# Copying the keys and summaries of every query tile on ScalarE instead of VectorE

## The chip, the cores and the metric

The kernel runs on one core of a Trainium2 chip. The metric is the device time of one execution in microseconds (us), taken as a median over runs. Differences are judged against that median. Engines are named as the profile names them: PE is TensorE's matmuls and PEld its weight loads, DVE is VectorE, ACT is ScalarE, POOL is GpSimd, SP is SyncE, whose queue issues most DMAs.

## The reference

Three layers run one after the other: an attention over a local window plus block summaries, a gated feed-forward layer, and a mixture of eight experts with a fixed capacity.

```
k_sum = k.reshape(B, H, nb, block, D).max(axis=3)          # block = 32
v_sum = v.reshape(B, H, nb, block, D).mean(axis=3)
scores_l = scale * q @ k^T, kept where |pos_q - pos_k| < 16, else -1e9
scores_s = scale * q @ k_sum^T + log(block)
a = softmax(concat[scores_l, scores_s])                    # over both kinds of keys
x = a @ concat[v, v_sum]

h = x @ w_in                                               # 512 -> 2048
x = (h * clip(h + 3, 0, 6) / 6) @ w_out                    # 2048 -> 512

logits = x @ w_gate                                        # 8 experts, 192 tokens each
assigned by falling logit, each expert up to its capacity
out[tokens of e] = relu(x @ w1[e]) @ w2[e]
```

B = 2, H = 8, 768 positions, head size 64, all in float32. The change touches the attention only.

## The kernel before, in words

**Query tiles.** The 1536 tokens are cut into twelve tiles of 128 queries, n = 0 to 11; tiles 0 to 5 are batch 0. For each batch the keys are transposed once into `kT` (two heads on 128 partitions, four such pairs, 768 positions), and `ks` holds the 24 block maxima. A tile is worked in two groups of 64 queries. Each group sees a window of 96 keys (its own 64 and 16 on each side) and all 24 summaries, 120 keys together. `window(n)` puts these 120 columns side by side into `kw` for each pair of heads and each group: two copies of keys of 4 x 96 columns a partition, and two of summaries of 4 x 24. At the ends of a batch (tiles 0, 5, 6 and 11) one window is cut short, its copy is smaller, and a memset fills the rest. Tile 0 is prepared in two halves of two pairs each. `qT` and `kw` have one buffer each.

**One step of the attention** handles half the heads of a tile (h = 0 or 1). `front` multiplies `qT` by `kw` on PE (line 372), then DVE adds the mask and takes the maximum, four times (line 380), and scales it (line 382). `soften` takes four exponentials on ACT (line 392, each with the sum of its row), DVE adds a small number to the sums and inverts them (lines 394 and 395), and POOL scales the weights `A` (line 396). Two steps later `turn` transposes `A` on PE (line 404) and ACT takes the result out of PSUM (line 406); `values` multiplies by the values on PE (line 419), and ACT and DVE split the result into an upper and a lower part of `x` (lines 437 and 77). In the second step of a tile the next one is prepared: `q_prep` transposes its queries on PE (line 338) and ACT copies `qT` (line 340), and then `window` fills `kw`.

**The first feed-forward product** (`gemm1`) runs for units of three tiles. Per block of 128 hidden columns twelve matmuls (lines 587 to 589) fill one of two PSUM banks; ACT takes the relu (line 590), DVE the gate (line 601), and that frees the bank. The weights come as 8-byte floats; DVE makes 4-byte floats of them in three instructions per block (line 268), ACT copies the upper part (line 285) and POOL subtracts (line 286). These conversions run during the first unit.

**What sets the order.** Instructions are issued to each engine in the order of the program and executed in that order. `drive` merges several generators: it always lets the one go on that is least far by planned costs (the numbers after `yield`), between a start and an end given as shares. First the preparation of batch 0 with tiles 0 to 2 beside the first conversions; then `gemm1` of unit u beside the attention of unit u + 1; after that the second product, the routing and the experts, in which no query tile is prepared.

Of the kernel before, what the change touches and what calls it, by code (L numbers as in the profile page):

```python
# [11 lines left out]
AF = mybir.ActivationFunctionType  # L12
# [7 lines left out]
WIN = QG + 2 * W  # L20
# [67 lines left out]
def build(ctx, tc, q, k, v, w_in, w_out, w_gate, w1, w2, out):  # L88
    nc = tc.nc
    PE, ACT, DVE, POOL, SP = nc.tensor, nc.scalar, nc.vector, nc.gpsimd, nc.sync  # L90
# [46 lines left out]
    kT = att.tile([128, HP, S], FT)  # L137
    ks = att.tile([128, HP, NB], FT)
# [205 lines left out]
    def window(n, hps=slice(0, HP)):  # L344

        i = n % 6
        kw = fr[n][1][:, hps]
        if i in (0, 5):
            for g in range(2):
                lo = i * 128 + g * QG - W  # L350
                a, z = max(lo, 0), min(lo + WIN, S)
                if z - a < WIN:
                    DVE.memset(kw[:, :, g, :W] if a > lo else kw[:, :, g, WIN - W:WIN], 0.0)
                DVE.tensor_copy(kw[:, :, g, a - lo:z - lo], kT[:, hps, a:z])
        else:
            for g in range(2):
                lo = i * 128 + g * QG - W
                DVE.tensor_copy(kw[:, :, g, :WIN], kT[:, hps, lo:lo + WIN])
        for g in range(2):
            DVE.tensor_copy(kw[:, :, g, WIN:], ks[:, hps])  # L360

    def front(n, h, after):
        b, i = divmod(n, 6)
        qT, kw = fr[n]
        A = Abuf[(2 * n + h) % (LAG + 1)]
        sp = [bank(0), bank(1)]
        for pr in range(2):
            hp = 2 * h + pr
            for g in range(2):
                for s in range(2):  # L370
                    r, c = slice(64 * s, 64 * s + 64), slice(QG * g, QG * g + QG)
                    PE.matmul(sp[s][c, pr * KEYS:(pr + 1) * KEYS], qT[r, hp, c], kw[r, hp, g], start=True, stop=True)
        if after:
            q_prep(n + 1)
        mk = mask[:, 0 if i == 0 else 2 if i == 5 else 1]
        sm = att.tile([128, 4, 4], FT, name="sm", bufs=2)
        for pr in range(2):
            for s in range(2):
                c = 2 * pr + s
                DVE.tensor_tensor_reduce(out=A[:, c], in0=sp[s][:, pr * KEYS:(pr + 1) * KEYS], in1=mk, scale=1.0,  # L380
                                         scalar=-3e38, op0=OP.add, op1=OP.max, accum_out=sm[:, 0, c:c + 1])
        DVE.tensor_scalar(sm[:, 1], sm[:, 0], -SCALE, None, op0=OP.mult)
        if after:
            window(n + 1)
        later.append((A, sm))
# [57 lines left out]
    def halves():  # L443
        for n in range(NT):
            b, i = divmod(n, 6)
            if b and i == 0:
                for g in range(2):
                    vsum(b, g)
                yield from kprep(b)
                zone()  # L450
                q_prep(n)
                window(n)
                yield 2400
# [286 lines left out]
    def prologue():  # L740
        for g in range(2):
            for i, c in enumerate(kprep_first(g)):
                yield c
                if g == 1 and i == 1:
                    yield next(attention)
                warm(1)
            warm((2, 8)[g])
            q_prep(0, range(2 * g, 2 * g + 2))
            window(0, slice(2 * g, 2 * g + 2))
            yield 450  # L750
            if g == 0:
                yield next(attention)
        yield from attend_unit(0)
# [71 lines left out]
    g = [0.0] + [RATIO ** i for i in range(J - 1)]  # L825
# [396 lines left out]
```

## Time and profile before

| what | value |
|---|---|
| median of 3 runs | 602.12 us (601.99 to 603.04) |
| profiled execution | 600.1 us, its span 598.2 us |
| busy, PE | 551.2 us, 92% of the span |
| busy, DVE | 400.6 us, 67% |
| busy, ACT | 288.8 us, 48% |
| busy, POOL | 178.2 us, 30% |
| mean granted TensorE clock | 0.981 of full |

The shares are averages over stages with different limits, so they don't tell which engine a stage waits for. The span runs from the first instruction to the last; the 1.9 us beside it lie around them. The query tiles are prepared between 8.9 us and 176 us of the span, twelve times. In a timeline a row is one instruction, or several of a kind merged, with its start, its duration, its engine and its line; in brackets stands how long the engine had been idle before and what it waited for. Neighbours on an engine overlap a little, so the distance between two starts is shorter than the first one's duration.

### The profile page before, as it was taken

What the parts mean: (1) busy time and instruction counts of PE and PEld (TensorE: products, weight loads), DVE (VectorE), ACT (ScalarE), POOL (GpSimd) and SP (SyncE); (2) the same over time, 40 slices, a digit from 0 to 9 for tenths busy, and PEclk for the clock granted to TensorE, in tenths of its full rate; (3) what the DMA queues carried; (4) which work ended last, traced back from release to release, by engine and by line L of the source; (5) the groups of instructions that cost most, each with busy time, mean ns of one, the idle gap of its engine ahead of it and who ended that gap; (6) DMA issues with size and microseconds to landing.
All of it is one profiled execution on the core that took longest, in us unless ns stands there. A gap on an engine that the chain in (4) does not pass through costs nothing.

```text
span 598.2 us, 10910 instructions
## 1 busy us (share of the span) xinstructions
PE 551.2 (92%) x3811; PEld 466.8 (78%) x3811; DVE 400.6 (67%) x1215; ACT 288.8 (48%) x694; POOL 178.2 (30%) x204
## 2 busy tenths in 40 slices
PE   7679778989999999899999898899999999999994
PEld 6558667878899999776687676678789889988883
DVE  6898994555534399961037787762588888888880
ACT  4376453435645455641131131133577677776760
POOL 1444648111111034662243434545101101110111
PEclk9879998989999999999999999999999999999998
DMA  9985981202210245330060000003579879887811
GB/s 204 253 194 147 257 200 33 49 18 64 58 39 1 72 142 175 112 93 1 1 201 11 0 2 2 0 19 142 168 219 283 231 241 283 265 253 240 253 61 32
DMA packets 102400, 75.06 MB, mean 125 GB/s; under 512 B 47488, under 2 KB 88448, under 8 KB 101952
## 3 DMA queue, kind: packets, MB, share of 16 engines
q1 hardware_dynamic: 100352, 67.96, 41.8%
q0 software_dynamic: 1984, 6.32, 2.9%
q8 instruction: 32, 0.52, 0.4%
q14 instruction: 32, 0.26, 0.1%
HBM read 67.55 MB, written 6.71 MB: 124 GB/s over the span
## 4 chain that ended last, share of the span: by engine, by line
PE 39%; issue 27%; DVE 23%; DMA 4%; POOL 3%; ACT 2%; SPq 1%; POOLq 0%; ACTq 0%; DVEq 0%
PE bank L587 7%; PE bank L588 6%; PE bank L589 6%; DVE t L268 5%; PE bank L704 3%; PE bank L705 3%; PE bank L706 3%; DVE big L889 3%; POOL out_dram L1025 2%; PE bank L894 2%; DVE x L529 2%; PE bank L613 2%; DMA t<-in_q_dram 2%; PE bank L419 1%; DVE A L380 1%
## 5 line engine op out<-in xcount | busy, mean ns | idle before, releaser
L587 PE MATMUL bank<-x,wh 128*128 128x384 f32 x256 | 92.4, 361 | 9.5 <-DVE t L601 9.3
L295 DVE TENSOR_TENSOR wl<-t,wh 128x1024 fp32r<-128x1024 f32 x64 | 77.0, 1221 | 20.5 <-ACT wh L294 18.1
L681 ACT ACTIVATE work<-t 128x384 fp32r<-128x384 f32 (+2 forms) x80 | 36.4, 459 | 107.5 <-PE bank L705 101.2
L589 PE MATMUL bank<-x,wl 128*128 128x384 f32 x256 | 87.4, 341 | 0.8 <-POOL wl L286 0.8
L588 PE MATMUL bank<-x,wh 128*128 128x384 f32 x256 | 87.1, 340 | 0.8 <-DVE x L77 0.8
L590 ACT ACTIVATE t<-bank,three 128x384 f32<-128x384 f32 x64 | 37.2, 581 | 94.1 <-PE bank L589 94.0
L682 POOL TENSOR_TENSOR tlx<-t,work 128x384 fp32r<-128x384 f32 (+1 forms) x52 | 56.8, 1094 | 84.2 <-ACT work L681 84.2
L704 PE MATMUL bank<-wh,work 128*128 128x512 f32 x192 | 78.0, 406 | 2.0 <-DVE t L601 2.0
L706 PE MATMUL bank<-wh,tlx 128*128 128x512 f32 x192 | 75.3, 392 | 0.1
L705 PE MATMUL bank<-wl,work 128*128 128x512 f32 x192 | 74.8, 390 | 0.0
L1050 PE MATMUL bank<-x,wh 128*128 128x384 f32 x256 | 73.7, 360 | 0.5 <-DVE x L976 0.5
L294 ACT ACTIVATE wh<-t 128x1024 fp32r<-128x1024 f32 x64 | 65.6, 1047 | 0.0
L1052 PE MATMUL bank<-x,wl 128*128 128x192 f32 x256 | 64.2, 251 | 0.0
L601 DVE SCALAR_TENSOR_TENSOR t<-t,bank 128x384 f32<-128x384 f32 x64 | 34.7, 548 | 40.0 <-ACT t L590 40.0
L396 POOL TENSOR_TENSOR A<-A,sm 128x480 f32<-128x480 f32 x24 | 24.2, 1010 | 119.0 <-ACT at L406 74.9
L587 PEld LDWEIGHTS bank<-x,wh 128*128 128x128 f32 x256 | 48.9, 191 | 13.4 <-DVE t L601 5.9
L1025 POOL DMA_INDIRECT out_dram<-t,idx x16 | 14.9, 930 | 141.6 <-DVE t L1074 136.1
L588 PEld LDWEIGHTS bank<-x,wh 128*128 128x128 f32 x256 | 49.1, 192 | 1.4 <-DVE x L77 1.4
L589 PEld LDWEIGHTS bank<-x,wl 128*128 128x128 f32 x256 | 48.9, 191 | 1.2 <-POOL wl L286 1.2
L1052 PEld LDWEIGHTS bank<-x,wl 128*128 128x128 f32 x256 | 48.9, 191 | 0.3
L1066 PE MATMUL bank<-wh,t 128*128 128x512 f32 x128 | 49.0, 392 | 0.0
L1050 PEld LDWEIGHTS bank<-x,wh 128*128 128x128 f32 x256 | 48.1, 188 | 1.2 <-DVE x L976 0.8
(182 smaller groups left out, 1088.9 us busy)
## 6 DMA issues: line engine op xcount, KB each, us to landing
t<-in_moe_w_dram SPq DMA_DIRECT2D x128, 256.0 KB
t<-in_moe_w_in_dram SPq DMA_DIRECT2D x16, 512.0 KB
big<-in_moe_w_out_dram SPq DMA_DIRECT2D x16, 512.0 KB
VW<-in_v_dram SPq DMA_DIRECT2D x20, 192.0 KB
t<-in_v_dram SPq DMA_DIRECT2D x4, 768.0 KB
t<-xs SPq DMA_DIRECT2D x8, 258.0 KB
raw<-in_q_dram SPq DMA_DIRECT2D x8, 256.0 KB
t<-in_k_dram SPq DMA_DIRECT2D x12, 128.0 KB
```

The source lines that it names most:

```text
L294: ACT.activation(hi, x, AF.Copy)
L295: DVE.tensor_tensor(lo, x, hi.bitcast(FT), op=OP.subtract)
L587: PE.matmul(p, wh[:, kk, :], xh[:, kk, :], start=kk == 0, stop=False)
L588: PE.matmul(p, wh[:, kk, :], xl[:, kk, :], start=False, stop=False)
L589: PE.matmul(p, wl[:, kk, :], xh[:, kk, :], start=False, stop=kk == KD - 1)
L682: (DVE if placed[0] else POOL).tensor_tensor(ths[i][1], t, ths[i][0].bitcast(FT), op=OP.subtract)
L704: PE.matmul(acc[j], th[:, c], WH[s], start=f == 0, stop=False)
L705: PE.matmul(acc[j], th[:, c], WL[s], start=False, stop=False)
L706: PE.matmul(acc[j], tl[:, c], WH[s], start=False, stop=f == NF - 1)
L1050: PE.matmul(p, a[:, kk, :], xt[:, kk].rearrange("p c s -> p (c s)"), start=kk == 0, stop=False, skip_group_check=True)
L1052: PE.matmul(p[:, :CAP], b[:, kk, :], xt[:, kk, 0, :], start=False, stop=kk == KD - 1, skip_group_check=True)
L1066: PE.matmul(p, x, w, start=m == 0 and i == 0, stop=m == NM - 1 and i == 2)
```

## The change

The copies that fill `kw` move from DVE to ACT, with the same sources, targets and sizes. The memset of a window that is cut short stays on DVE. Nothing else is edited.

```
                 if z - a < WIN:
                     DVE.memset(kw[:, :, g, :W] if a > lo else kw[:, :, g, WIN - W:WIN], 0.0)
-                DVE.tensor_copy(kw[:, :, g, a - lo:z - lo], kT[:, hps, a:z])
+                ACT.activation(kw[:, :, g, a - lo:z - lo], kT[:, hps, a:z], AF.Copy)
         else:
             for g in range(2):
                 lo = i * 128 + g * QG - W
-                DVE.tensor_copy(kw[:, :, g, :WIN], kT[:, hps, lo:lo + WIN])
+                ACT.activation(kw[:, :, g, :WIN], kT[:, hps, lo:lo + WIN], AF.Copy)
         for g in range(2):
-            DVE.tensor_copy(kw[:, :, g, WIN:], ks[:, hps])
+            ACT.activation(kw[:, :, g, WIN:], ks[:, hps], AF.Copy)
```

The order of PE's instructions is the same as before, and DVE's and ACT's differ in these copies alone. ACT's queue at the start, from the second half of tile 0 to the exponentials that follow the preparation of tile 1 (`kT` are the transposed keys, `bank_...` PSUM tiles, `A` the weights):

```order
 L308 ACTIVATE kT<-bank_223 128x2x2x128
 L340 ACTIVATE qT<-bank_241 128x256
+L354 ACTIVATE kw<-kT 128x2x80
+L354 ACTIVATE kw<-kT 128x2x96
+L360 ACTIVATE kw<-ks 128x2x24 x2
 L340 ACTIVATE qT<-bank_263 128x512
+L358 ACTIVATE kw<-kT 128x4x96 x2
+L360 ACTIVATE kw<-ks 128x4x24 x2
 L392 ACTIVATE A_90,sm<-A_90,sm 128x120 x4
```

Tile 1's copies now stand behind its `qT` and ahead of the exponentials of the step before it.

ACT's queue at the preparation of tile 3, where line 285 is the upper part of a converted weight block:

```order
 L406 ACTIVATE at<-bank_459 120x512
 L340 ACTIVATE qT<-bank_477 128x512
+L358 ACTIVATE kw<-kT 128x4x96 x2
+L360 ACTIVATE kw<-ks 128x4x24 x2
 L285 ACTIVATE wh<-t 128x512
 L392 ACTIVATE A_91,sm<-A_91,sm 128x120 x4
```

The four copies come ahead of the weight copy and the exponentials.

DVE's queue at the preparation of tile 5, the last one of batch 0, with the end of a step's maxima ahead and a conversion behind:

```order
 L380 ISA sm 128x1
 L382 TENSOR_SCALAR sm<-sm 128x4
-L354 COPY kw<-kT 128x4x96
 L353 MEMSET kw 128x4x16
-L354 COPY kw<-kT 128x4x80
-L360 COPY kw<-ks 128x4x24 x2
 L268 TENSOR_SCALAR t<-t 128x512
 L268 SCALAR_TENSOR_TENSOR t<-t 128x512 x2
```

After the scaled maxima only the memset is left ahead of the conversion.

## Rows read from the trace of the kernel before

**Rows 1.** Busy time by stretch: us, PE, PEld, DVE, ACT, POOL, PEclk, DMA share, GB/s.

```profile
48.00:92.00 44.00, 35.05 (x306) 30.58 (x305) 41.23 (x98) 23.16 (x64) 23.20 (x17) 1.00 0.84 193
92.00:200.00 108.00, 104.38 (x891) 94.63 (x892) 51.25 (x211) 52.37 (x160) 25.51 (x26) 0.97 0.16 36
```

**Rows 2.** Groups by line, shapes apart, VectorE to 200 us: copies into kw.

```profile
L358 DVE COPY kw<-kT 128x384 f32<-128x384 f32 x16 | 4.9, 347 | 0.0
...
L360 DVE COPY kw<-ks 128x96 f32<-128x96 f32 x22 | 3.5, 198 | 0.0
L354 DVE COPY kw<-kT 128x320 f32<-128x320 f32 x3 | 1.9, 623 | 0.0
```

**Rows 3.** Groups by line, shapes apart, ScalarE: copies in SBUF.

```profile
L681 ACT ACTIVATE work<-t 128x384 fp32r<-128x384 f32 x48 | 25.0, 524 | 86.3 <-PE bank L705 83.8 <-PE bank L706 2.4
...
L681 ACT ACTIVATE work<-t 128x128 fp32r<-128x128 f32 x16 | 4.7, 306 | 4.3 <-PE bank L705 3.3 <-DVE tlx L682 0.8
```

**Rows 4.** Timeline at tile 1: start us, us, engine line, idle before.

```profile
19.84 1.12 PE L338 MATMUL bank<-ident,t 128*128 128x128 f32 x4 [3.29 <-DMA t<-in_q_dram]
...
21.56 0.39 ACT L392 ACTIVATE A<-A,sm 128x120 f32<-128x120 f32 x1
...
23.20 0.17 DVE L394 TENSOR_SCALAR sm<-sm 128x4 f32<-128x4 f32 x1 [1.14 <-ACT A L392]
...
24.09 0.28 DVE L380 CUSTOM_DVE_ANT_0 A<-bank,mask 128x120 f32<-128x120 f32 x1 [0.27 <-issue]
```

**Rows 5.** Timeline at tile 2.

```profile
29.90 0.60 ACT L340 ACTIVATE qT<-bank 128x512 f32<-128x512 f32 x1 [0.62 <-PE bank L338]
...
30.93 0.40 ACT L392 ACTIVATE A<-A,sm 128x120 f32<-128x120 f32 x1 [0.43 <-DVE sm L382]
...
33.31 0.16 DVE L394 TENSOR_SCALAR sm<-sm 128x4 f32<-128x4 f32 x1
...
33.56 1.12 PE L419 MATMUL bank<-at,VW 120*64 120x64 f32 x16 [1.28 <-ACT at L406]
```

**Rows 6.** Timeline at tile 3.

```profile
38.62 0.62 ACT L285 ACTIVATE wh<-t 128x512 fp32r<-128x512 f32 x1
...
39.14 0.39 ACT L392 ACTIVATE A<-A,sm 128x120 f32<-128x120 f32 x1
...
41.26 0.16 DVE L394 TENSOR_SCALAR sm<-sm 128x4 f32<-128x4 f32 x1
```

**Rows 7.** Timeline at tile 4.

```profile
44.91 0.58 ACT L340 ACTIVATE qT<-bank 128x512 f32<-128x512 f32 x1
...
45.79 0.60 ACT L437 ACTIVATE x<-bank 128x512 fp32r<-128x512 f32 x1 [0.30 <-PE bank L419]
...
46.81 0.68 DVE L77 TENSOR_TENSOR x<-bank,x 128x512 fp32r<-128x512 f32 x1
...
47.55 0.45 PE L588 MATMUL bank<-x,wh 128*128 128x384 f32 x1 [0.56 <-DVE x L77]
```

**Rows 8.** Timelines at tile 5, and where line 268 takes long.

```profile
59.46 3.16 POOL L286 TENSOR_TENSOR wl<-t,wh 128x512 fp32r<-128x512 f32 x2
...
61.46 1.35 DVE L354 COPY kw<-kT 128x320 f32<-128x320 f32 x1
...
62.96 0.42 DVE L268 TENSOR_SCALAR t<-t 128x512 int32<-128x512 int32 x1
...
82.82 1.48 DVE L268 TENSOR_SCALAR t<-t 128x512 int32<-128x512 int32 x1
```

**Rows 9.** Timeline at tile 7.

```profile
119.67 0.58 ACT L340 ACTIVATE qT<-bank 128x512 f32<-128x512 f32 x1
...
120.94 0.58 ACT L590 ACTIVATE t<-bank,three 128x384 f32<-128x384 f32 x1 [0.69 <-PE bank L589]
...
122.14 0.65 PE L372 MATMUL bank<-kw,qT 64*64 64x120 f32 x16
```

**Rows 10.** Busy time of one stretch, columns as in Rows 1.

```profile
95.00:98.00 3.00, 3.00 (x12) 2.90 (x12) 1.11 (x2) 1.71 (x4) 2.86 (x2) 0.50 0.00 0
```

## The prediction

> **What bounds the kernel now.** I read the table by stretch first. Up to 92 us VectorE is the engine that is never free: in 48 to 92 us it is busy 41.23 of 44 us while TensorE works 35.05 of them; from 92 to 200 us it is the other way round, TensorE 104.38 of 108 and VectorE 51.25 [rows 1]. After 200 us no query tile is prepared any more, so the change can only shift that part. So whatever the change does to the time happens in the first 92 us, and there I went through the timelines of ScalarE, VectorE and TensorE tile by tile.
>
> **What is moved, and its price.** Each of the twelve tiles has two copies of keys and two of summaries. On VectorE they are 347 and 198 ns long [rows 2], 1.09 us a tile, about 0.77 us with the overlap of neighbours. On ScalarE no such copy stands in the trace. The nearest rows are the copies on line 681: 524 ns for 384 columns, 306 ns for 128 [rows 3]; that is 0.85 ns a column, so 279 ns for the 96 columns of a summary. Neighbours on ScalarE overlap by 0.1 us: a copy of 0.62 us starts at 38.62 and the next instruction at 39.14 [rows 6]. So a tile's four copies hold ScalarE for 0.42 + 0.42 + 0.18 + 0.18 = 1.20 us. As bounds: 0.77 us, if they cost what VectorE's do, and 1.66 us without any overlap.
>
> VectorE's copies stand behind the four reductions of a step, so nothing but VectorE's next work waits there. ScalarE's stand between the copy of qT and the four exponentials of the same step, and everything after these in its queue is late by 1.20 us unless it had to wait anyhow. Behind the exponentials wait VectorE (line 394, the row sums), then GpSimd's scaling, then TensorE's transposes. So I replay the tiles one by one.
>
> **Tile 0.** Both halves are done while tile 1's queries are on their way: TensorE stood 3.29 us for that transfer until 19.84 [rows 4]. The eight small copies, about 1.7 us on ScalarE together by the same slope, end before it. Price 0; without that cover 1.7 us.
>
> **Tile 1.** Its qT depends on that transfer, and the four copies are now queued behind it. VectorE had made them earlier, while everybody waited. The exponentials start at 21.56 + 1.20 = 22.76, and VectorE's line 394, at 23.20 before, at 24.40. Before, VectorE lost 0.27 us after it to an unexplained wait and started the second reduction only at 24.09 [rows 4]; with everything later TensorE is further ahead there, and I count about 0.8 us of lateness instead of 1.2.
>
> **Tile 2.** With 0.8 us of lateness qT starts at 30.70, the copies run to 32.40, and the exponentials start there instead of at 30.93: 1.47 later. Of the 1.47, 0.8 is the old lateness; the rest of the copies fits into the 0.43 us that they waited for VectorE before and what overlaps. Four exponentials and line 394 took 1.64 us at tile 1 (21.56 to 23.20), so line 394 goes to about 34.05, against 33.31 [rows 5]. VectorE has lost its own 0.77 us of copies and just stands idle instead. Lateness on VectorE stays 0.75. But the transposed weights leave ScalarE 1.47 late, and TensorE waited for exactly these at 33.56 (1.28 us, to ScalarE's line 406) [rows 5]; a small gap behind takes some of it back and TensorE goes on about 1.2 late.
>
> **Tile 3.** qT follows TensorE and is 1.2 late; the tile's copies add 1.20. So the weight copy of line 285, which stands next, starts at 41.0 instead of 38.62 and the exponentials at 41.5 instead of 39.14. They started without any wait before [rows 6]: here the full 1.20 shows. Line 394 comes at about 43.15 instead of 41.26 [rows 6], 1.9 late. VectorE's conversions ahead of it no longer fill the time.
>
> **Tile 4.** The 1.9 us are carried to qT (44.91, now 46.8). Copies to 48.5, and only then the upper half of x on line 437, which started at 45.79. It is ready at 49.1, VectorE's subtraction on line 77 starts at 49.15 instead of 46.81, and TensorE waits for that with its first large product: 47.55 becomes 49.9 [rows 7]. The first large product of the program starts **2.35 us late**. Bounds for the four tiles together: 0.8 (tile 1 alone, the others hidden) and 4.8 (four times 1.20).
>
> **Tile 5.** This is the tile that VectorE is rid of while it is the bound. The second copy of keys took 1.35 us there, beside a GpSimd subtraction running from 59.46 to 62.62; its like took 0.26 us each at the two other places (three of mean 623 ns, less the long one) [rows 2, 8]. So the tile cost VectorE 0.77 us and 1.1 us of waiting. The gain is 1.9 us if that wait is gone with the copy, or 0.77 if the next VectorE instruction inherits it. The next is a conversion on line 268 that took 0.42 us here, and 1.48 us at 82.82 [rows 8]. I take **0.85 gained**, near the lower end.
>
> The Trainium skill, "SBUF — State Buffer", section "SBUF: two separate sides", says that VectorE's two-port operations and GpSimd share one pair of ports as an exclusive lock, so that the later one is blocked until the other instruction ends, and that ScalarE has ports of its own. By that rule the copies on ScalarE are never held, and VectorE's next two-port instruction is held in their place: the gain would be 0.77, which gives a sum 0.1 us higher. The 1.48 us row agrees with it; no row shows the copies on ScalarE.
>
> **Tiles 6 to 11.** TensorE is the bound. qT and copies take 0.50 + 1.20 us from qT's start. The tightest place is tile 7: qT at 119.67, kw then ready at 121.5, TensorE asked for it at 122.14 [rows 9]. The relu on line 590, 120.94 before, starts 0.43 later there; it frees a bank that TensorE wants only after the next column tile of some 2 us. Price 0; without that cover six times 0.43, 2.6 us. Below zero: TensorE was idle 3.6 us in 92 to 200 us [rows 1], so no more than that could be won.
>
> **The sum.** 2.35 − 0.85 + 0 = +1.5 us. The profiled execution took 600.1 us (span 598.2 and 1.9 around it), so its like would take 601.6. The median of the timed runs, 602.12, lies 2.0 above the profiled one, and the forecast for the median is 603.6 us.
>
> **Rivals.**
> *The clock takes more.* TensorE ran at half its speed, 1.2 instead of 2.4 GHz, in 95 to 98 us [rows 10], shortly after a stretch in which VectorE was the bound and TensorE idle for a fifth of the time [rows 1]. With the longer waits at tiles 3 and 4 the first large products might run so too. Three such microseconds at half speed cost 1.5 us: 605.1. For it: longer gaps on TensorE before 50 us. Against: it ran at full speed all through 48 to 92 us, gaps and all [rows 1].
> *It is taken back.* The start loses 2.35, but VectorE's wait at tile 5 really goes (1.9): +0.45, 602.6, no change that can be told. For it: GpSimd's second subtraction there waits for a copy on ScalarE that also starts later, so that the two may miss each other. Against: GpSimd's work is no less, and what it misses there it can meet further on.
> *VectorE's relief wins.* The copies on ScalarE run while VectorE is still at its four reductions, as they start as soon as qT does, and the exponentials lose nothing; VectorE gains 0.77 us at tiles 2, 3 and 4 and 0.85 at tile 5. Together −3.2, and the loss of tile 1 (0.8) stays: 599.7, faster. It decides where qT is finished more than 1.2 us before the maxima are. At tile 2 the room is 0.53 us (30.40 to 30.93), at tile 3 none [rows 5, 6].
> *Nothing moves.* That the copies stay on VectorE is excluded by the order of its instructions.
>
> **Chances.** Forecast 0.50 (its own range 602.6 to 605.0), the clock 0.15, taken back 0.23, relief 0.12. Differences below 0.2% (1.2 us) can't be told from no change. Of the forecast's half I put 0.42 above 1.2 us; with the clock that is 0.57 slower. Same: 0.08 and nearly all of "taken back", 0.30 together. Faster: the relief and a rest, 0.13. The range, which leaves out most of the relief and the clock's far end, is 600.9 to 606.0.
>
> **What the profile after would show.** ScalarE's copies of keys near 0.52 and of summaries near 0.28 us. Exponentials of tiles 2 and 3 starting right behind a summary copy, and VectorE's line 394 waiting for ScalarE, some 2 us at tile 3. The first product of line 588 at 49 to 50.5 us instead of 47.55, and everything in the stretch that VectorE bounds one to two us late at its end. After 95 us the same distance all the way. I am wrong if line 588 starts at 48.5 or earlier, if the distance changes after 95 us by more than 1 us, or if the stretch 50 to 93 us shrinks by over 2 us.

## The result and the profile after

| what | before | after |
|---|---|---|
| median of 20 runs each | 602.68 us (601.1 to 607.32) | **606.14 us** (603.86 to 609.86) |
| profiled execution, its span | 600.1, 598.2 us | 606.0, 604.2 us |
| busy, VectorE | 400.6 us | 389.6 us |
| busy, ScalarE | 288.8 us | 302.1 us |
| mean granted TensorE clock of the profiled run | 0.981 | 0.972 |

The ratio is 1.0064, 95% interval 1.0048 to 1.0079: slower, by some 3.5 to 3.9 us, where 1.5 were forecast. The time lies 0.14 us above the range. The direction and the place are the forecast's; the size is not. Ratios and means of runs, here and below, leave out runs more than 1.5% above the fastest of their kernel: one of the kernel before in three of the four comparisons below, and one of the run called e12, whose +2.0 us would be +2.6 with it.

The copies themselves cost what was read for them. Groups by line of the profile after, ScalarE, shapes apart (busy us, mean ns of one, idle before); they answer to [rows 2] and to the copies of [rows 3], which the forecast took in their place:

```profile
L358 ACT ACTIVATE kw<-kT 128x384 f32<-128x384 f32 x16 | 7.4, 516 | 0.0
L360 ACT ACTIVATE kw<-ks 128x96 f32<-128x96 f32 x22 | 4.9, 275 | 0.0
```

516 and 275 ns, where 524 and 279 were taken from line 681. The stretches of [rows 1] after the change, and one more, the 14 us from the moment at which tile 1's queries have landed (us, PE, PEld, DVE, ACT, POOL, PEclk, DMA share, GB/s):

```profile
20.91:34.91 14.00, 13.11 (x92) 11.27 (x92) 6.89 (x24) 5.98 (x23) 5.47 (x7) 0.52 1.02 232
48.00:92.00 44.00, 35.34 (x314) 30.27 (x313) 37.66 (x99) 27.56 (x87) 20.50 (x16) 0.96 0.87 205
92.00:200.00 108.00, 103.54 (x887) 93.34 (x886) 51.52 (x191) 58.42 (x182) 28.52 (x27) 0.97 0.16 36
```

The first row is the surprise. In its 14 us TensorE got 0.52 of its clock, which is nearly all of them at 1.2 GHz, and finished 92 matmuls. Before, the same 14 us looked like this:

```profile
19.84:33.84 14.00, 11.28 (x133) 9.20 (x135) 12.22 (x42) 7.98 (x30) 5.87 (x8) 0.87 1.13 271
```

133 matmuls at 0.87. The third row after the change, from 92 us, is as the forecast had it: TensorE is still the bound and the clock the same 0.97.

What happens at tile 1 stands in the timeline after (start us, us, engine line, in brackets idle before and what it waited for), and answers to [rows 4]:

```profile
20.91 1.12 PE L338 MATMUL bank<-ident,t 128*128 128x128 f32 x4 [4.11 <-DMA t<-in_q_dram]
...
22.13 0.60 ACT L340 ACTIVATE qT<-bank 128x512 f32<-128x512 f32 x1 [6.00 <-PE bank L338]
22.62 0.93 ACT L358 ACTIVATE kw<-kT 128x384 f32<-128x384 f32 x2
23.45 0.44 ACT L360 ACTIVATE kw<-ks 128x96 f32<-128x96 f32 x2
23.77 1.23 PE L372 MATMUL bank<-kw,qT 64*64 64x120 f32 x16 [0.89 <-ACT kw L360]
23.80 0.38 ACT L392 ACTIVATE A<-A,sm 128x120 f32<-128x120 f32 x1
...
25.44 0.17 DVE L394 TENSOR_SCALAR sm<-sm 128x4 f32<-128x4 f32 x1 [3.97 <-ACT A L392]
...
25.97 0.28 DVE L380 CUSTOM_DVE_ANT_0 A<-bank,mask 128x120 f32<-128x120 f32 x1
```

The queries landed 1.07 us later in this run (20.91 against 19.84). The change has no part in that: in another profile of the changed kernel (e1) they landed at 19.84. Counted from that moment, VectorE's line 394 comes after 4.53 us instead of 3.36: 1.17 late, the copies' 1.18 us (22.62 to 23.80). The second reduction on line 380 comes after 5.06 us instead of 4.25, only 0.81 late, since the 0.27 us of waiting ahead of it are gone. ScalarE had stood idle for 6.00 us just ahead of qT. At tile 3, answering to [rows 6], the exponentials again stand behind the copies, with the weight copy of line 285 between, and VectorE and TensorE wait for ScalarE:

```profile
42.05 0.58 ACT L340 ACTIVATE qT<-bank 128x512 f32<-128x512 f32 x1
42.53 0.93 ACT L358 ACTIVATE kw<-kT 128x384 f32<-128x384 f32 x2
43.35 0.44 ACT L360 ACTIVATE kw<-ks 128x96 f32<-128x96 f32 x2
43.70 0.62 ACT L285 ACTIVATE wh<-t 128x512 fp32r<-128x512 f32 x1
44.22 0.38 ACT L392 ACTIVATE A<-A,sm 128x120 f32<-128x120 f32 x1
...
45.86 0.17 DVE L394 TENSOR_SCALAR sm<-sm 128x4 f32<-128x4 f32 x1 [1.14 <-ACT A L392]
...
46.84 0.69 PE L419 MATMUL bank<-at,VW 120*64 120x64 f32 x16 [2.06 <-ACT at L406]
```

And at tile 4, answering to [rows 7], the upper half of x waits behind the copies, and TensorE's first large product for it:

```profile
51.93 0.58 ACT L437 ACTIVATE x<-bank 128x512 fp32r<-128x512 f32 x1
...
52.54 0.69 DVE L77 TENSOR_TENSOR x<-bank,x 128x512 fp32r<-128x512 f32 x1 [1.81 <-ACT x L437]
...
53.29 0.44 PE L588 MATMUL bank<-x,wh 128*128 128x384 f32 x1 [0.28 <-DVE x L77]
```

53.29 instead of 47.55. Less the 1.07 us of the late queries that is 4.7 late, twice the forecast's 2.35. But not all of it is the copies' doing. In the profile of e4, one of the runs described below, whose kernel is the kernel before up to tile 5, the queries landed at 19.87 and the same product came at

```profile
51.46 0.44 PE L588 MATMUL bank<-x,wh 128*128 128x384 f32 x1 [0.28 <-DVE x L77]
```

which is 3.9 us late with none of the copies on ScalarE. Between landing and this product TensorE's mean clock was 0.82 in the kernel before, 0.69 in e4 and 0.74 in the changed kernel. That is 10.0, 19.6 and 16.8 us at 1.2 GHz. From the first two, 3.9 us for 9.6, the clock's part of the 4.7 us can be estimated at some 2.8, and about 2 are left for the copies, near the forecast's 2.35.

At tile 5 the forecast's gain is seen on VectorE. Timelines of VectorE and GpSimd after, answering to [rows 8]:

```profile
65.19 3.24 POOL L286 TENSOR_TENSOR wl<-t,wh 128x512 fp32r<-128x512 f32 x2
...
66.62 0.32 DVE L382 TENSOR_SCALAR sm<-sm 128x4 f32<-128x4 f32 x1
...
67.32 2.39 DVE L268 SCALAR_TENSOR_TENSOR t<-t 128x512 int32<-128x512 int32 x2
69.63 0.55 DVE L601 SCALAR_TENSOR_TENSOR t<-t,bank 128x384 f32<-128x384 f32 x1
...
80.23 0.43 DVE L268 TENSOR_SCALAR t<-t 128x512 int32<-128x512 int32 x1 [0.40 <-DMA t<-in_moe_w_in_dram]
...
86.17 0.73 DVE L268 TENSOR_SCALAR t<-t 128x512 int32<-128x512 int32 x1 [0.71 <-DMA t<-in_moe_w_in_dram]
```

From line 382 to the gate on line 601 VectorE takes 3.01 us, before 3.86 (60.89 to 64.75):

```profile
60.89 0.32 DVE L382 TENSOR_SCALAR sm<-sm 128x4 f32<-128x4 f32 x1
...
63.41 1.42 DVE L268 SCALAR_TENSOR_TENSOR t<-t 128x512 int32<-128x512 int32 x2
64.75 0.55 DVE L601 SCALAR_TENSOR_TENSOR t<-t,bank 128x384 f32<-128x384 f32 x1
```

0.85 us, as forecast, and the conversion did inherit the wait for GpSimd: two instructions of line 268 took 2.39 us, where the same two took 1.42 before. The rows at 80.23 and 86.17 show something else that is new: VectorE waits for weights to arrive, 1.4 us in three waits, where it waited for none before. Whether the gain is handed back there is looked at further on.

### The profile page after: what moved, and what is told of

Read it like the earlier page. It is cut to its first block, busy times and chain, and to the rows that moved or that the text cites. A ratio compares the mean times of both kernels' runs of the same rounds, so it can differ in the third digit from the quotient of the medians.

```text
span 604.2 us, 10918 instructions
## 1 busy us (share of the span) xinstructions
PE 554.8 (92%) x3811; PEld 470.2 (78%) x3811; DVE 389.6 (64%) x1163; ACT 302.1 (50%) x746; POOL 177.9 (29%) x204
## 4 chain that ended last, share of the span: by engine, by line
PE 42%; issue 26%; DVE 16%; DMA 5%; ACT 4%; POOL 4%; SPq 1%; POOLq 0%; ACTq 0%; DVEq 0%
PE bank L587 7%; PE bank L589 6%; PE bank L588 6%; PE bank L704 4%; PE bank L705 3%; PE bank L706 3%; DVE big L889 3%; POOL out_dram L1025 2%; DVE t L268 2%; PE bank L894 2%; DMA t<-in_q_dram 2%; PE bank L613 2%; DMA t<-in_moe_w_in_dram 2%; PE bank L419 2%; PE bank L372 2%
## 5 line engine op out<-in xcount | busy, mean ns | idle before, releaser
L601 DVE SCALAR_TENSOR_TENSOR t<-t,bank 128x384 f32<-128x384 f32 x64 | 34.8, 549 | 42.7 <-ACT t L590 42.6
```

## The experiments

**The theories.** Q: the place in ScalarE's queue costs, since the copies stand ahead of exponentials that others wait for, and nothing else does. C: on top of that, TensorE runs at 1.2 GHz for longer once it has been made to wait, so a wait costs more than its own length. N: the difference is within what two sets of runs differ by.

**How the runs are read.** Every timed run lists its span and its mean granted clock. 2 x (1 - clock) x span counts TensorE's time at 1.2 GHz, the lower of its two levels. Over all 298 runs, compared only within one kernel, a microsecond of it goes with 0.30 us of span (error 0.015); that is what goes together, not yet what causes what. The table gives, for each kernel, the mean span less that of the kernel before in the same comparison (standard errors 0.5 to 0.8 us, here called errors), and the time at 1.2 GHz (errors 0.8 to 2.3 us; the kernel before had 32.9, 32.8, 32.6 and 30.9 us in the four comparisons).

| run | copies on ScalarE | ratio, 95% interval | span, us | at 1.2 GHz, us |
|---|---|---|---|---|
| e1 | all, as changed | 1.0091 (1.0065 to 1.0117) | +4.0 | 36.7 |
| e2 | tile 1 | 1.0042 (1.0014 to 1.0071) | +2.1 | 38.2 |
| e3 | tiles 2 to 4 | 1.0049 (1.0020 to 1.0078) | +1.9 | 34.4 |
| e4 | tile 5 | 1.0011 (0.9989 to 1.0033) | 0.0 | 33.8 |
| e8 | tiles 6 to 11 | 1.0007 (0.9973 to 1.0040) | +0.3 | 32.8 |
| e7 | all, ahead of qT | 1.0009 (0.9979 to 1.0039) | +0.2 | 31.7 |
| e12 | all, tile 1 ahead of qT | 1.0033 (1.0002 to 1.0064) | +2.0 | 32.6 |
| e13 | all, tiles 2 to 4 ahead of qT | 1.0023 (1.0004 to 1.0042) | +1.9 | 35.1 |
| e9, e14 | all but tile 1 | 1.0060 (1.0026 to 1.0094), 1.0056 (1.0027 to 1.0084) | +3.3, +3.9 | 35.7, 34.8 |
| e5 | none, idle matmuls | 0.9984 (0.9950 to 1.0019) | -1.3 | 24.8 |
| e6 | all, idle matmuls | 1.0020 (0.9987 to 1.0052) | +1.3 | 26.1 |
| e10 | all, ahead of qT, idle matmuls | 0.9984 (0.9955 to 1.0013) | -1.3 | 23.1 |
| e11 | some, idle matmuls | 0.9972 (0.9942 to 1.0003) | -1.9 | 24.3 |

The changed kernel in the first comparison: +3.3 us, 37.4 us at 1.2 GHz (20 runs, against e1's kernel before).

**e1: the changed kernel again**, no edit.

> The changed kernel once more, unedited. Its first profile showed a half-speed stretch of TensorE of 13.7 us from 20.8 us on (3.4 us before) and tile 1's query transfer landing 1.07 us later. Theory Q+C (late exponentials, and a TensorE that is then slow): the long slow stretch is there again, the first large product comes about 5 us after 47.55 counted from the same landing of the queries, ratio 1.005 to 1.008. Theory Q alone (the queue, the long slow stretch was chance): the slow stretch at 20 us is 3.4 to 7 us, the first large product about 2.4 us late, ratio 1.003 to 1.005. Theory N (all but noise): ratio within 1.002.

It is slower again, with an interval that lies above 1.006. N is out. Its profile has the long slow stretch again (a clock of 0.51 in the 14 us after the landing) and the first large product 4.6 us late, as Q+C expected.

**e2 to e4 and e8: one part each.** In all of them `window` fills kw through `put`, and `ON_ACT` names the tiles that go to ScalarE. Against the kernel before:

```
+        put = (lambda d, x: ACT.activation(d, x, AF.Copy)) if n in ON_ACT else DVE.tensor_copy
...
-                DVE.tensor_copy(kw[:, :, g, :WIN], kT[:, hps, lo:lo + WIN])
+                put(kw[:, :, g, :WIN], kT[:, hps, lo:lo + WIN])
...
-    LAG = 2
+    LAG, ON_ACT = 2, (1,)    # e2;  e3: (2, 3, 4);  e4: (5,);  e8: range(6, 12)
```

> Tile 1 alone is copied on ScalarE, all others on VectorE. Theory Q+C: VectorE's line 394 at tile 1 comes 1.2 us later, TensorE waits for kw, the slow stretch from 20 us on is 10 us or longer, and the first large product comes 3 to 4 us late: ratio about 1.005. Theory Q alone: 0.8 to 1.2 us late, ratio 1.0015. If tile 1 is free, as the transfer hides it: ratio 1.000.

> Tiles 2, 3 and 4 alone are copied on ScalarE. Theory Q+C: tile 1 is as before, slow stretch of 3.4 us at 20 us, and lateness only from the exponentials of tiles 3 and 4: first large product 1 to 2 us late, ratio 1.002 to 1.003. If every late exponential makes TensorE slow, a long slow stretch appears after 30 us and the first large product is 3 us late, ratio 1.005. If VectorE's relief wins here: first large product 1 to 2 us earlier, ratio 0.997.

> Tile 5 alone is copied on ScalarE. It lies where VectorE is the bound. Theory Q: VectorE's next gate after these copies comes 0.85 us earlier and the end of the stretch that VectorE bounds too; ratio 0.9985. If VectorE's next instruction inherits the whole wait for GpSimd and the relu is late, nothing: 1.000.

> Tiles 6 to 11 alone are copied on ScalarE, where TensorE is the bound. Theory Q: nothing changes, ratio 1.000, the distance between the gates after 95 us as before. If the relus that start 0.4 us later hold TensorE's banks: up to 2.6 us more, ratio 1.004.

2.1 + 1.9 + 0.0 + 0.3 = 4.3 us, with an error near 1.4, against +3.3 and +4.0 for the whole: the loss is made at tiles 1 to 4, in two like halves. No gain shows at tile 5, though its 0.85 us aren't excluded by an error of 0.6. Of tile 1's 2.1 us some 1.6 go with the clock (5.3 us more at 1.2 GHz, times 0.30). At tiles 2 to 4 TensorE has 1.5 us more at 1.2 GHz, within the errors. e2 lies nearer to Q+C than to Q, e4 and e8 at the expectation of no change. e3's mean span, +0.3%, is at the upper end of Q+C; its ratio would fit the rival in which every late exponential makes TensorE slow, but its profile shows no long slow stretch after 30 us.

**e5 and e6: TensorE kept busy** while it waits for tile 1's queries, in the kernel before and in the changed one. The matmuls' result isn't read.

```
         if after:
-            q_prep(n + 1)
+            warm(14 if n == 0 else 0), q_prep(n + 1)
```

> The kernel before, with 14 idle matmuls (128 x 128, result unused) on TensorE between the first products of tile 0 and tile 1's query transposes, where it stands some 3 us for the transfer. Over all runs so far a microsecond of half-speed TensorE costs 0.29 us of time, and the kernel before has about 33 us of it. Theory C (a TensorE that stands there is slow afterwards): the half-speed stretch that starts near 19 us is gone, total slow time falls by 5 to 10 us, time by 1.5 to 3 us, ratio 0.995 to 0.9975. If the slow stretch is chance: slow time as before, ratio 1.000 to 1.001.

> The changed kernel with the same 14 idle matmuls at the same place. Theory Q+C: what is left of the loss is the late exponentials alone, 2.2 us at equal clock: ratio to before 0.998 to 1.001, and to the warmed kernel before about 1.0035. If the changed kernel's extra slow time has another cause: ratio still 1.005 or more. Theory that the clock is all of it: as fast as the warmed kernel before, 0.995 to 0.997.

They have 8 and 11 us less at 1.2 GHz, as C asked, and both spans fall, by 1.3 us (with an interval of the ratio that still touches 1) and by 2.0 to 2.7. Both ratios lie between the ranges of the theories. Between the two kernels 2.6 us remain with nearly the same clock (24.8 and 26.1 us). So C has a share, and Q keeps the larger one. The microsecond at 1.2 GHz that these matmuls take away is worth less than the 0.30: 0.16 us (1.3 of 8.0, with an error of some 0.1) and 0.18 to 0.25. Below, the clock's share is given by both 0.16 and 0.30.

**e7: the copies ahead of qT.** Same copies, same engine; only their place in ScalarE's queue is another.

```
         if after:
-            q_prep(n + 1)
+            (n + 1 in KEYS_FIRST) and (tiles(n + 1), window(n + 1)), q_prep(n + 1)
...
-        if after:
+        if after and n + 1 not in KEYS_FIRST:
             window(n + 1)
...
-    LAG = 2
+    KEYS_FIRST = range(1, 12); LAG, ON_ACT = 2, range(12)     # KEYS_FIRST in e12: (1,);  e13: (2, 3, 4)
```

(`tiles` reserves `qT` and `kw` of a tile, which `q_prep` did before.)

> All copies on ScalarE as in the changed kernel, but for tiles 1 to 5 and 7 to 11 ahead of the copy of qT instead of behind it, so that they run while TensorE transposes the queries. Theory Q: at tile 1 they are done before the queries land, at tiles 2 and 3 ScalarE was idle there (1.1 us before qT at tile 3) and the exponentials are at most 0.2 us late, only tile 4 keeps its 1.2 us: ratio 0.999 to 1.002. If it is ScalarE's load or the slower copy itself and not the place: 1.005 to 1.007.

Its timeline at tile 1:

```profile
17.84 0.94 ACT L345 ACTIVATE kw<-kT 128x384 f32<-128x384 f32 x2 [0.81 <-ACT kw L345]
18.68 0.44 ACT L345 ACTIVATE kw<-ks 128x96 f32<-128x96 f32 x2
...
21.41 0.60 ACT L340 ACTIVATE qT<-bank 128x512 f32<-128x512 f32 x1 [2.29 <-PE bank L338]
21.90 0.39 ACT L392 ACTIVATE A<-A,sm 128x120 f32<-128x120 f32 x1
...
23.55 0.17 DVE L394 TENSOR_SCALAR sm<-sm 128x4 f32<-128x4 f32 x1 [1.09 <-ACT A L392]
```

(Line 345 is that of `put`.) The copies are done while everybody waits, the exponentials start right behind qT, and line 394 comes 3.29 us after the landing (20.26), as before the change. The loss is gone, +0.2 with an error of 0.6, as Q expected. So within that error ScalarE's copies cost nothing by their length; their place costs.

**e9 and e14: all but tile 1.** `ON_ACT` is every tile except 1.

> Every tile's copies on ScalarE except those of tile 1, which stay on VectorE. If the parts add up (tile 1 alone gave +2.1 us of mean span, tiles 2 to 4 +1.9, tile 5 0.0, tiles 6 to 11 +0.3), this gives +1.6 to +2.2 us over the kernel before, a ratio near 1.003, with some 34 us of TensorE time at half speed. If the loss belongs to the exponentials of any one late tile, whichever comes first, then tile 2 takes tile 1's place as the first late one: +3.5 us, a ratio near 1.006, and some 37 us at half speed.

> The kernel with all copies but tile 1's on ScalarE a second time, since +3.3 us with an error near 0.8 lay between the two expectations. Sum theory: +1.6 to +2.2 us, which with the first result would average some 2.6. Latest-wait theory: +3.3 us again.

Both came out at the whole loss, which speaks against a sum. The timeline of VectorE and GpSimd in e9 at tile 1 shows why this kernel doesn't isolate what it was meant to:

```profile
17.75 0.62 DVE L358 COPY kw<-kT 128x384 f32<-128x384 f32 x2
18.29 2.48 DVE L360 COPY kw<-ks 128x96 f32<-128x96 f32 x2
18.30 5.47 POOL L186 TENSOR_TENSOR t<-t 96x1024 f32<-96x1024 f32 x5 [1.88 <-DMA t<-in_v_dram]
20.69 3.65 DVE L183 TENSOR_REDUCE t<-t 96x64 f32<-96x2048 f32 x1
...
24.27 0.15 DVE L394 TENSOR_SCALAR sm<-sm 128x4 f32<-128x4 f32 x1
```

and that of e14:

```profile
18.78 2.77 DVE L358 COPY kw<-kT 128x384 f32<-128x384 f32 x2
18.80 5.61 POOL L186 TENSOR_TENSOR t<-t 96x1024 f32<-96x1024 f32 x5 [1.35 <-DMA t<-in_v_dram]
21.48 1.39 DVE L360 COPY kw<-ks 128x96 f32<-128x96 f32 x2
```

against the kernel before:

```profile
18.14 0.32 DVE L360 COPY kw<-ks 128x96 f32<-128x96 f32 x2
18.38 3.68 DVE L183 TENSOR_REDUCE t<-t 96x64 f32<-96x2048 f32 x1
18.64 5.43 POOL L186 TENSOR_TENSOR t<-t 96x1024 f32<-96x1024 f32 x5 [1.36 <-DMA t<-in_v_dram]
```

GpSimd's five additions of line 186 start when values arrive. In the kernel before they start after VectorE's copies are over. In e9 and e14 they start beside them, and VectorE's copies, 0.32 and 0.62 us long otherwise, are held to 2.48 and 2.77. Line 394 comes 4.64 and 6.34 us after the landing, as late as in the changed kernel or later. So tile 1 was late here too, by another way, and these two runs neither show nor refute a sum.

**e12 and e13: ahead of qT for some tiles only.** There tile 1's copies stay on ScalarE, which no row shows held.

> All copies on ScalarE, and only those of tile 1 ahead of the copy of qT; tiles 2 to 11 stand as in the changed kernel. Sum theory: tile 1's place in the queue costs about 2 us wherever it stands, so this comes out at +1.3 to +2 us of mean span over the kernel before, a ratio near 1.003. Latest-wait theory: the lateness of the tiles doesn't add, tiles 2 to 4 alone make the loss of the whole; then it is +3 us or more, a ratio near 1.0055, as without tile 1 on ScalarE at all.

> All copies on ScalarE, those of tiles 2 to 4 ahead of the copy of qT, tile 1 and tiles 5 to 11 as in the changed kernel. Sum theory: what is left is tile 1's share and little beside it, +2 us over the kernel before, a ratio near 1.0035. Latest-wait theory: tile 1's 1.1 us of lateness alone cost something only as long as nothing later is late; here nothing is, so also +2 us. A share below 1 us (ratio under 1.002) would say that tile 1 matters only together with the tiles behind it.

+2.0 and +1.9: taking tile 1's lateness away leaves 2, taking that of tiles 2 to 4 away leaves 2. That speaks for the sum theory. The latest-wait theory asked for +3 or more in e12 and, by the same reasoning, in e3, which had +1.9. With errors of 0.8 each, the two together make it unlikely but don't rule it out. The clock goes with tile 1: 1.7 us more at 1.2 GHz than in the kernel before in e12 (within the errors), 4.2 in e13.

**e10 and e11: towards a faster kernel.** e10 is e7 with e5's line. e11 also leaves tiles 0, 1, 4 and 6 on VectorE, and of the others only 2 and 3 are copied ahead of qT. Against e10:

```
-    KEYS_FIRST = range(1, 12); LAG, ON_ACT = 2, range(12)
+    KEYS_FIRST = (2, 3); LAG, ON_ACT = 2, (2, 3, 5, 7, 8, 9, 10, 11)
```

> All copies on ScalarE, but those of tiles 1 to 11 ahead of the copy of qT, and fourteen idle 128x128 matmuls on TensorE while it waits for the queries of tile 1. The result is still the reference's. If the loss is the place in ScalarE's queue plus TensorE time at half speed, both are gone here: as with the kernel before with the same matmuls (1.3 us under the kernel before), 600.5 to 602 us against 602.7, a ratio of 0.997 to 1.000, with some 25 us at half speed. If copies on ScalarE cost something beyond their place in the queue, it stays at the plain keys-first version's distance or above: 1.001 or more.

> As the run before it, but tiles 0, 1, 4 and 6 go back to VectorE, which has nothing else to do there; on ScalarE stay tiles 2 and 3 (ahead of qT), 5 and 7 to 11. If VectorE's relief is worth something anywhere, it is at tiles 2, 3 and 5: 0.3 to 1.5 us below the kernel before with the idle matmuls alone, a ratio of 0.995 to 0.998. If tile 5's gain is lost again to the arrival of the weights, as in the trace of the changed kernel, it is the ratio of the idle matmuls alone, 0.998.

With the idle matmuls the three kernels line up: none moved -1.3, moved -1.3 if ahead of qT, +1.3 if behind it. So the 2.6 us (error 0.8) go with the place in the queue. A part of them may come by the clock: e6 has 3.0 us more at 1.2 GHz than e10, which is 0.5 to 0.9 us. e11 has the lowest time of all (median 601.11 against 603.35 us), but its interval still touches 1, and against e5 it differs by 0.6 us with an error of 0.9. A gain of VectorE's relief is not shown.

## Why the forecast was right in kind and wrong in size

**Right.** The prices of the copies (the upper bound of a tile's four copies, 1.66 us, should read 1.61; nothing hangs on it); tile 0 at nothing, though no run tests it by itself; the mechanism at tiles 1, 3 and 4, in the order and with the waits foretold, but line 394's wait for ScalarE at tile 3 is 1.14 us and not some 2; the inherited wait at tile 5. By the Trainium skill, "SBUF — State Buffer", section "SBUF: two separate sides", ScalarE never waits for the ports that VectorE and GpSimd share, and a two-port instruction of VectorE is blocked while GpSimd has them. The trace agrees (ScalarE's 16 large copies took 511 to 522 ns, two of line 268 2.39 us), and so do e9 and e14, where VectorE's own copies are held to 2.48 and 2.77 us. Tiles 6 to 11 cost +0.3 with an error of 0.7, forecast 0. From 100 to 253 us the gates on line 601 come 5.0 to 5.5 us later than in the kernel before, and a stretch at a clock of 0.69 from 260 to 265 us (1.00 before) makes it 5.9.

**The step that failed: tile 1, whose "about 0.8 us of lateness" went into the sum as its whole price, with TensorE's clock unchanged.** The lateness itself was right. The 0.27 us were taken back, and VectorE's second reduction is 0.81 us late in the changed kernel's profile, 0.71 in e1, 0.81 in e2. But the price of tile 1 was some 2.0 us (e2 +2.1, e13 +1.9; the whole less e12, 3.3 to 4.0 less 2.0, is 1.3 to 2.0). TensorE's clock, put at nothing in the sum, is half of the difference or more. Leaving out those with idle matmuls and e9 and e14, the kernels in which tile 1's copies stand behind qT (the changed one, e1, e2, e13) spend 35.1 to 38.2 us at 1.2 GHz, those in which they don't (the kernel before, e3, e4, e7, e8, e12) 30.9 to 34.4. The middles, 36.9 and some 32.8 us, are 4 us apart, which is 0.6 us at 0.16 and 1.2 us at 0.30. What is left of e2 and e13 without their extra time at 1.2 GHz (5.3 and 4.2 us) is 0.5 to 1.2 us, around the forecast's 0.8. Where it happens is seen in the 14 us after the landing. The granted clock there is 0.51 to 0.58 in all four profiles with the late tile 1. With tile 1 in time it is 0.87 or 0.88 in the kernel before, e3, e8 and e12, but 0.55 and 0.53 in e4 and e7:

```profile
19.87:33.87 14.00, 14.00 (x111) 12.14 (x112) 9.38 (x32) 5.61 (x21) 5.66 (x7) 0.55 1.04 254
```

This is e4, which is the kernel before up to tile 5. So the slow stretch comes without the lateness too; the lateness makes it likelier. Four of four profiles against two of six are few, and it is the mean times at 1.2 GHz that carry this. The profile on which I built the forecast was one without. Its clock, 0.981, was above the 0.973 that 32.6 us at 1.2 GHz in a span of 601 come to. I added the 2.0 us between that profile and the median as a constant; by its 22.7 us at 1.2 GHz against 32.6, such time accounts for 1.6 to 3.0 us, so for most or all of it. "The clock takes more" was a rival with 0.15, put at the first large products near 50 us and argued away because the clock was full from 48 to 92. The same trace shows TensorE at 1.2 GHz ahead of that, with us, PE, PEld, DVE, ACT, POOL, PEclk, DMA share, GB/s in a row:

```profile
33.50:36.00 2.50, 2.26 (x24) 1.74 (x28) 2.43 (x13) 1.08 (x7) 0.99 (x1) 0.50 0.99 182
36.00:40.00 4.00, 4.00 (x40) 2.96 (x40) 3.80 (x19) 2.90 (x12) 1.93 (x2) 0.50 0.77 202
```

The clock belongs to the time between TensorE's wait for the queries and the first large product, and it was a term of the sum.

**The term beside it: tile 5, "0.85 gained".** Seen to the hundredth in the trace, and worth 0.0 with an error of 0.6 in e4's time. From the first large product to 100 us the changed kernel won back 0.5 us on the kernel before in its profile, and 0.0 in e1's; e4 won 0.1. It is tempting to blame VectorE's new waits for weights, 1.4 us in the changed kernel and 1.9 in e4. But e8, whose copies are on VectorE at tile 5 as before, has 2.0 us of them, and lost 0.6 us over the same stretch:

```profile
75.99 0.43 DVE L268 TENSOR_SCALAR t<-t 128x512 int32<-128x512 int32 x1 [1.33 <-DMA t<-in_moe_w_in_dram]
...
81.50 0.82 DVE L268 TENSOR_SCALAR t<-t 128x512 int32<-128x512 int32 x1 [0.62 <-DMA t<-in_moe_w_in_dram]
```

So the waits come without the gain too, and no run shows that it is lost to them. What failed is the step from 0.85 us on VectorE to 0.85 us of time: I had asked what the next VectorE instruction inherits and not what the last one of the stretch waits for. Where the gain goes stays open.

**Tiles 2 to 4: 1.55 forecast** (2.35 less 0.8), +1.9 (e3) and +2.0 (e12) measured: right within the errors.

So 2.0 + 1.9 + 0.0 + 0.3 = 4.2, with an error near 1.4, stands for the forecast's 0.8 + 1.55 - 0.85 + 0 = 1.5, and the whole measured 3.3 to 4.0. The rivals "taken back" and "VectorE's relief wins" did not happen; line 588 at 53.29 us lay outside the 49 to 50.5 that I had named. What else stays open is why e4 and e7 got the slow stretch with tile 1 in time.

## What to carry to other kernels

An instruction moved to an engine that is half idle is cheap or dear by what stands behind it in that engine's queue: put it ahead of the instruction that waits for a transfer, not behind. When a change makes TensorE wait longer early on, price the clock as a term of its own, and compare the profile's mean clock with that of the timed runs before taking its durations as typical. With the same instructions up to there and another clock, the profiles of e4 and of the kernel before are 4 us apart at the first large product. A gain that a trace shows on the engine that bounds a stretch is not yet a gain in time: ask what the last instruction of the stretch waits for, its inputs' arrival among others.

## What the runs showed of the hardware that I had not expected

The idle matmuls (fourteen in the code, recorded as 28) fill 3.39 us in which TensorE would have waited for a transfer, and took 8 to 11 us off its time at 1.2 GHz. The 14 us after the landing in e10, and what was done just ahead of it:

```profile
17.31 3.39 PE L148 MATMUL bank<-ident 128*128 128x128 f32 x28
20.94 0.66 PE L338 MATMUL bank<-ident,t 128*128 128x128 f32 x4 [0.23 <-DMA t<-in_q_dram]
```

```profile
20.94:34.94 14.00, 10.61 (x145) 8.61 (x146) 11.91 (x45) 9.16 (x35) 6.25 (x8) 1.00 1.14 259
```

Full clock and 145 matmuls, where the changed kernel did 92. It isn't certain, either: with the same matmuls the clock of these 14 us was 0.76 in e5, 0.63 in e6 and 0.76 in e11.

The second is chance at tile 1. VectorE's copies meet GpSimd's line 186 when its transfer lands before they are over, and a meeting costs 2.2 us on the copies of 0.32 us. Of the eight profiles with these copies on VectorE three show it (e5, e9, e14). In e5 everything up to there is the kernel before but for the idle matmuls, so the kernel before seems to carry that risk. e9 and e14 are the only two of the eight with tile 0's copies on ScalarE, which may have a part in it; no run separates that. No profile with tile 1 on ScalarE shows a copy held.
